# Making the rests of w1 and w2 with TensorE and ScalarE, and their signs with GpSimd, in a kernel of top-32 attention and a gated product

## The chip, the core and the metric

The kernel runs on one core of a Trainium2 chip. The metric is the time of one execution in microseconds (us) on the device. The engines are called PE (TensorE; PEld is its loading of weights), DVE (VectorE), ACT (ScalarE), POOL (GpSimd) and SP (SyncE, which issues the transfers here).

## The reference

```python
# q, k, v: (8, 8, 576, 64); x: (4608, 512); w1, w2: (512, 1024); w3: (1024, 1024); w_out: (1024, 512)
scores = q @ k^T / sqrt(64)
kth = np.partition(scores, -32, axis=-1)[..., -32:-31]
scores = np.where(scores >= kth, scores, -1e9)
attn = softmax(scores)                       # only the 32 largest of a row count
x = (attn @ v).transpose(0, 2, 1, 3).reshape(B * S, H * D)
out = ((x @ w1) * (x @ w2) @ w3) @ w_out
```

All inputs are random. The matrices w1, w2, w3 and w_out are handed to the device as 64-bit numbers, and the kernel turns them into 32-bit ones itself.

## The kernel before

**Slots.** The attention is cut into 144 slots, 18 for each of the 8 batches; a slot holds 128 rows of queries of two heads. The main loop takes slots through a software pipeline: in one turn of the loop PE makes the scores `st` of slot p+1, DVE finds the 32 largest of each row of slot p (`top`, working copy `w`), POOL and ACT mask and exponentiate slot p-1 (`edge`, `pab`, `sums`), and PE turns (`tp`, `ro`) and multiplies with the values (`ro`) for slot p-2. Each engine works through its instructions in the order in which the program states them.

**The product.** When the last slot of a part of a batch is through, its columns `xf` go through the four matrices: `moe_steps` states matmuls `ab` (x by w1 and w2) and `eo` (by the fold of w3 and w_out). Each matrix product is made of three: high part by high part, high by rest, rest by high. `fill(n)` states some 29 of these matmuls in a turn, at three places, and what is left over stands behind the last slot. `moe_steps` can't go on past `while done[f // 4] < NFC` before the weights of that half are there.

**Loading the weights.** Forty units of 128 x 512 numbers come in at the start: 8 of w_out, 16 of w3, 16 of w1 and w2. `startup` lists their order, and `warm` states one step of up to five units under way at up to four places of a turn, so the loading lies between the first slots. A unit's `decode` makes, from the upper words `high` of the 64-bit numbers, the shifted exponent and mantissa, and from the lower words `low` the last bits `r`. ACT does both conversions, DVE puts sign and shifted bits together in `y` (`scalar_tensor_tensor`), and POOL adds `r` (`y<-y,z`, or `wo<-y,z` for w_out). Where the flag `by_pool` is set, POOL made the signs into `y` first (`y<-z`); where it isn't, DVE did (`tensor_scalar`, `y<-t`). For w1 and w2 it isn't set. Behind that, `load_w12` has ACT copy `y` to the high part `wh`, and POOL subtracts for the rest `wl`. `load_w3` hands eight PE products (`pf`) to a list `heavy`, from which `weigh` states one or eight at two places of a turn.

**Memory.** The pool `ps_m` has three banks of PSUM; `ab`, `eo`, `pf` and the `t` of `decode` share them. `z` (the 64-bit numbers) has four buffers, and `y` and `xf` share nine. PE and ACT read PSUM's other banks for `st`, `tp` and `ro`.

All instructions go through a helper, so that nearly every row of the profile has line L52; the names tell them apart.

Of the kernel before, what the change touches and what calls it, by code (L numbers as in the profile page):

```python
# [9 lines left out]
F32 = mybir.dt.float32  # L10
F32R = mybir.dt.float32r
I32 = mybir.dt.int32
U16 = mybir.dt.uint16
AF = mybir.ActivationFunctionType
ALU = mybir.AluOpType
# [45 lines left out]
def attn_moe(ctx: ExitStack, tc: tile.TileContext, q, k, v, w1, w2, w3, w_out, out, flag, general):  # L61
# [11 lines left out]
    nc = tc.nc  # L73
    pe, act, dve, pool, sp = nc.tensor, nc.scalar, nc.vector, nc.gpsimd, nc.sync

    const = ctx.enter_context(tc.tile_pool(name="const", bufs=1))
# [9 lines left out]
    ps_m = ctx.enter_context(tc.tile_pool(name="ps_m", bufs=3, space=PSUM))  # L86

    ident = const.tile([128, 128], F32, name="ident")
    make_identity(nc, ident)
    coef = const.tile([128, 2, 2], F32, name="coef")  # L90
    pool.memset(coef[:, :, 0:1], -SCALE)
    pool.memset(coef[:, :, 1:2], STEEP)
# [11 lines left out]
    if not general:  # L104
        pe, act, dve, pool, sp = (InOrder(tc, e) for e in (pe, act, dve, pool, sp))
# [7 lines left out]
    def decode(z, by_pool, dst=None):  # L113

        y = x_p.tile([128, 2 * NA], F32, tag="x", name="y")[:, :512]
        high = z[:, 1:1024:2]  # L120
        low = z.bitcast(U16)[:, 1:2048:4]
        r, u = z[:, 0:1024:2].bitcast(I32), y.bitcast(I32)
        if by_pool:
            pool.tensor_scalar(y, high, 0.0, 1.0, op0=ALU.mult, op1=ALU.mult)
            yield
        t = ps_m.tile([128, 512], F32, tag="mm", name="t")
        act.activation(t, high, AF.Copy, scale=2.0**-112)
        act.activation(r, low, AF.Copy, scale=2.0**-13)
        yield
        ti = t.bitcast(I32)  # L130
        if not by_pool:
            dve.tensor_scalar(u, ti, -(2**31), None, op0=ALU.bitwise_and)
        dve.scalar_tensor_tensor(u, ti, 3, u, op0=ALU.logical_shift_left, op1=ALU.bitwise_or)
        yield
        dst = y if dst is None else dst
        pool.tensor_tensor(dst.bitcast(I32), u, r, op=ALU.add)
        yield
        return dst

    done = {"pf": 0, 0: 0, 1: 0}  # L140

    def load_w12(i, c, z):
        y = yield from decode(z, False)
        c, h = c // 2, c % 2
        if len(wl[i]) == h:
            while done["pf"] < NFC:
                yield
        if len(wl[i]) == h:
            wl[i].append(const.tile([128, half], F32R, tag="wl1", name="wl11"))
        y_hi, y_lo = wh[i][:, c * DF + h * 512 : c * DF + (h + 1) * 512], wl[i][h][:, c * 512 : (c + 1) * 512]  # L150
        act.copy(y_hi, y)
        yield
        pool.tensor_tensor(y_lo, y, y_hi.bitcast(F32), op=ALU.subtract)
        done[h] += 1

    def load_wout(c, z):
        yield from decode(z, c % 2, wo[:, c * 512 : (c + 1) * 512])

    fold, heavy = {}, []

    def weigh(n):
        while heavy and n:
            heavy.pop(0)()
            n -= 1

    def load_w3(c, z):
        f, i = c // 2, c % 2
        y = yield from decode(z, i)
        if i == 0:
            fold[f] = ps_m.tile([128, 512], F32, tag="mm", name=f"pf{f}")  # L170

        def product(j):
            pe.matmul(
                fold[f], y[:, (j % 4) * 128 : (j % 4 + 1) * 128], wo[:, j * DM : (j + 1) * DM],
                start=(j == 0), stop=(j == NFC - 1),
            )

        heavy.extend((lambda j=j: product(j)) for j in range(4 * i, 4 * i + 4))
        last = heavy[-1]
        if general:  # L180
            weigh(4)
        while last in heavy:
            yield
        if i == 1:
            cut = slice(f * DM, (f + 1) * DM)
            act.copy(wf[0][:, cut], fold[f])
            yield
            dve.tensor_tensor(wf[1][:, cut], fold[f], wf[0][:, cut].bitcast(F32), op=ALU.subtract)
            done["pf"] += 1
# [178 lines left out]
    def moe_steps(b, part, xs, after):  # L368
# [61 lines left out]
    thirds = [(w3[c], lambda z, c=c: load_w3(c, z)) for c in range(2 * NFC)]  # L430
    firsts = [
        (w[2 * c + h], lambda z, i=i, c=2 * c + h: load_w12(i, c, z))
        for h in range(2) for i, w in enumerate((w1, w2)) for c in range(NCC)
    ]
# [94 lines left out]
    for p in range(-1, n_slots + 3):  # L529
# [29 lines left out]
        if 0 <= j < n_slots:  # L559
            exps(edges[j], *pabs[j], 0)  # L560
            exps(edges[j], *pabs[j], 1)
        weigh(1)
        fill(SHARE[1])
        next(finder, None)
# [6 lines left out]
        if 0 <= m < n_slots:  # L571
            us, t = slots[m]
# [11 lines left out]
        if 0 <= j < n_slots:  # L584
            invert(pabs[j][1])
            normalise(*pabs[j])
        weigh(8)
        fill(SHARE[2])
        for _ in finder:
# [66 lines left out]
```

## Time and profile before

| | |
|---|---|
| time, median of 3 runs | 1272.27 us (1270.61 to 1272.45) |
| time of the profiled execution | 1272.79 us |
| its span, first to last instruction | 1270.8 us |
| mean granted TensorE clock, share of full | 0.988 |
| busy: PE / DVE / ACT / POOL | 1212.8 / 1135.0 / 942.9 / 870.2 us |

The time of an execution is 2.0 us longer than its span. A busy PE is not PE at its peak: matmuls are pipelined, and one that lasts 0.31 us may be followed by the next after half of that. So the text uses the distance from one start to the next where a price of PE is wanted.

### The profile page before, as it was taken

The page shows a single profiled execution, that of the slowest core. Times are in us where ns is not written, and L with a number is a line of the kernel's source. Part 1 is how long each engine was busy: PE and PEld are TensorE (multiplying, and loading weights), DVE is VectorE, ACT ScalarE, POOL GpSimd, SP SyncE. Part 2 cuts the span into 40 slices and gives each one's busy share as a digit, 9 for nine tenths or more (in the row PEclk, how much of TensorE's full clock was granted, in tenths as well). Part 3 has the DMA queues.
Part 4 walks back from the last instruction along what each step waited for, and adds up shares of the span by engine and source line. Part 5 has one row for each costly group of instructions (what it writes and reads, how often), then busy time and mean ns, then how long its engine had stood idle before and what let it go on. Part 6 is the DMA issues. An engine that isn't in the chain of part 4 may idle for free.

```text
span 1270.8 us, 29917 instructions
## 1 busy us (share of the span) xinstructions
PE 1212.8 (95%) x10513; PEld 1043.9 (82%) x10513; DVE 1135.0 (89%) x3968; ACT 942.9 (74%) x2025; POOL 870.2 (68%) x1213
## 2 busy tenths in 40 slices
PE   3788879999999999999999999999999999999998
PEld 1444468888888888888888888888888888888898
DVE  6898979999999999999999999999999999999910
ACT  6786767777777777777777777777777777777731
POOL 5887887676776667676676777676676767676731
PEclk9898989999999999999999999999999999999999
DMA  6444321212112021202112021202112111202000
GB/s 234 160 143 143 125 87 39 76 42 70 55 39 82 20 87 40 90 27 70 55 39 90 27 72 40 91 28 70 55 39 90 36 62 40 91 27 69 13 22 21
DMA packets 42803, 85.92 MB, mean 68 GB/s; under 512 B 4754, under 2 KB 21138, under 8 KB 42642
## 3 DMA queue, kind: packets, MB, share of 16 engines
q1 hardware_dynamic: 42642, 83.91, 20.3%
q8 instruction: 85, 1.39, 0.5%
q14 instruction: 76, 0.62, 0.2%
HBM read 74.45 MB, written 9.44 MB: 66 GB/s over the span
## 4 chain that ended last, share of the span: by engine, by line
PE 84%; POOL 8%; issue 2%; ACT 2%; DVE 2%; DMA 1%; SPq 0%; POOLq 0%; ACTq 0%; DVEq 0%
PE ab L52 31%; PE eo L52 16%; PE ro L52 14%; PE st L52 12%; PE tp L52 9%; POOL pab L52 4%; POOL y L52 2%; PE pf L52 2%; POOL wl L52 1%; DMA z<-in_wo 1%; ACT pab L52 1%; DVE w L52 1%; DVE top L52 1%; POOL g L52 0%; DVE y L52 0%
## 5 line engine op out<-in xcount | busy, mean ns | idle before, releaser
L52 POOL TENSOR_TENSOR pab<-s,pab 128x576 f32<-128x576 f32 x288 | 404.6, 1426 | 124.3 <-ACT pab L52 124.3
L52 DVE MAX8 top<-w 128x8 f32<-128x192 f32 (+1 forms) x1152 | 478.5, 448 | 0.0
L52 PE MATMUL ab<-xf,wh 128*128 128x256 f32 (+1 forms) x2048 | 438.9, 302 | 9.5 <-ACT asb L52 4.6
L52 PEld LDWEIGHTS ab<-xf,wh 128*128 128x128 f32 x2048 | 333.3, 189 | 21.0 <-issue 8.9
L52 ACT ACTIVATE pab<-s,edge 128x576 f32<-128x576 f32 x288 | 207.9, 770 | 174.9 <-POOL edge L52 174.9
L52 PE MATMUL ab<-xf,wl 128*128 128x256 f32 (+1 forms) x1024 | 307.6, 300 | 0.0
L52 DVE MATCH_REPLACE8 w<-top,w 128x192 f32<-128x192 f32 x864 | 289.7, 343 | 0.0
L52 POOL TENSOR_SCALAR pab<-pab,sums 128x576 f32<-128x576 f32 x288 | 211.7, 748 | 80.3 <-DVE sums L52 80.3
L52 ACT ACTIVATE pab<-pab,edge 128x576 f32<-128x576 f32 x288 | 223.2, 780 | 14.0 <-POOL pab L52 11.2
L52 PE MATMUL eo<-g,wf 128*128 128x256 f32 (+1 forms) x1536 | 231.6, 301 | 0.0
L52 PEld LDWEIGHTS eo<-g,wf 128*128 128x128 f32 x1536 | 208.5, 188 | 8.1 <-issue 7.5
L52 PEld LDWEIGHTS ab<-xf,wl 128*128 128x128 f32 x1024 | 193.5, 189 | 4.1 <-issue 4.1
L52 PE MATMUL st<-kt,qt 64*128 64x192 f32 (+3 forms) x1280 | 184.0, 436 | 11.4 <-DVE w L52 4.5
L52 ACT COPY pts<-tp 128x1024 f32<-128x1024 f32 x144 | 145.5, 1010 | 46.9 <-PE tp L52 44.5
L52 ACT COPY s<-st 128x768 f32<-128x768 f32 (+1 forms) x288 | 169.7, 645 | 0.0
L52 PEld LDWEIGHTS st<-kt,qt 64*128 64x128 f32 (+1 forms) x1280 | 98.2, 179 | 86.4 <-issue 18.7
L52 PE MATMUL tp<-ident,pab 128*128 128x128 f32 x1152 | 153.2, 277 | 15.5 <-POOL y L52 5.2
L52 DVE TENSOR_TENSOR w<-w,st 128x384 f32<-128x384 f32 x288 | 158.2, 549 | 4.9
L52 PE MATMUL ro<-pts,vt 128*64 128x128 f32 (+1 forms) x2560 | 161.6, 270 | 1.0 <-ACT pr L52 1.0
L52 DVE TENSOR_TENSOR w<-s,st 128x384 f32<-128x384 f32 x288 | 146.7, 551 | 14.0
L52 POOL TENSOR_TENSOR g<-whole,g 128x256 fp32r<-128x256 f32 (+1 forms) x128 | 103.0, 805 | 78.7 <-ACT g L52 78.7
L52 PEld LDWEIGHTS ro<-pts,vt 128*64 128x64 f32 x2560 | 127.9, 138 | 34.6 <-issue 24.0
(47 smaller groups left out, 1127.3 us busy)
## 6 DMA issues: line engine op xcount, KB each, us to landing
vt<-in_v SPq DMA_DIRECT2D x64, 352.0 KB, 3.1
kt<-in_k SPq DMA_DIRECT2D x64, 320.0 KB, 3.8
z<-in_w SPq DMA_DIRECT2D x32, 512.0 KB, 3.7
qt<-in_q SPq DMA_DIRECT2D x32, 160.0 KB, 3.1
out_t<-osb SPq DMA_DIRECT2D x32, 160.0 KB, 1.8
z<-in_wo SPq DMA_DIRECT2D x8, 512.0 KB, 5.8
qt<-in_q SPq DMA_DIRECT2D x32, 128.0 KB, 3.1
out_t<-osb SPq DMA_DIRECT2D x32, 128.0 KB, 1.7
```

What stands on the lines that cost most here:

```text
L52: ins = fn(*args, **kw)
```

## The change

The rest of a unit of w1 or w2 is no longer subtracted by POOL. A bank `rest` of `ps_m` receives two matmuls, the identity by `y` and a negated identity (`minus`, made once by ACT) by `wh`, and ACT copies `rest` to `wl`. The two matmuls go through `heavy`, like those of w3. The signs of w1 and w2 are made by POOL instead of DVE. And for all forty units ACT writes the converted upper words over themselves in `z` instead of into a bank `t`, so that `t` is gone and DVE reads `z`.

```diff
+    minus = const.tile([128, 128], F32R, name="minus")
+    nc.scalar.activation(minus, ident, AF.Copy, scale=-1.0)
...
-        t = ps_m.tile([128, 512], F32, tag="mm", name="t")
-        act.activation(t, high, AF.Copy, scale=2.0**-112)
+        act.activation(high, high, AF.Copy, scale=2.0**-112)
         act.activation(r, low, AF.Copy, scale=2.0**-13)
         yield
-        ti = t.bitcast(I32)
+        ti = high.bitcast(I32)
         if not by_pool:
             dve.tensor_scalar(u, ti, -(2**31), None, op0=ALU.bitwise_and)
         dve.scalar_tensor_tensor(u, ti, 3, u, op0=ALU.logical_shift_left, op1=ALU.bitwise_or)
...
     def load_w12(i, c, z):
-        y = yield from decode(z, False)
+        y = yield from decode(z, True)
...
         act.copy(y_hi, y)
         yield
-        pool.tensor_tensor(y_lo, y, y_hi.bitcast(F32), op=ALU.subtract)
+        rest = ps_m.tile([128, 512], F32, tag="mm", name="rest")
+
+        def subtract():
+            pe.matmul(rest, ident, y, start=True, stop=False)
+            pe.matmul(rest, minus, y_hi, start=False, stop=True)
+
+        heavy.append(subtract)
...
+        while subtract in heavy:
+            yield
+        act.copy(y_lo, rest)
         done[h] += 1
```

On POOL, this is the twelfth of the slots, between the `edge` of one slot and that of the next, before the change:

```order
L52 TENSOR_TENSOR edge<-top_100,coef 128x4
L52 TENSOR_TENSOR pab<-s,pab 128x576 x2
L52 TENSOR_TENSOR over<-top_100 128x2
L52 TENSOR_TENSOR wl_107<-y,wh_101 128x512
L52 TENSOR_TENSOR y<-y,z 128x512
L52 TENSOR_SCALAR sums<-sums 128x2
L52 TENSOR_TENSOR wl_107<-y,wh_101 128x512
L52 TENSOR_TENSOR y<-y,z 128x512
L52 TENSOR_SCALAR pab<-pab,sums 128x576 x2
```

and with the change:

```order
L52 TENSOR_TENSOR edge<-top_102,coef 128x4
L52 TENSOR_TENSOR y<-y,z 128x512
L52 TENSOR_TENSOR pab<-s,pab 128x576 x2
L52 TENSOR_TENSOR over<-top_102 128x2
L52 TENSOR_SCALAR y<-z 128x512
L52 TENSOR_TENSOR y<-y,z 128x512
L52 TENSOR_SCALAR sums<-sums 128x2
L52 TENSOR_SCALAR y<-z 128x512
L52 TENSOR_SCALAR pab<-pab,sums 128x576 x2
L52 TENSOR_TENSOR y<-y,z 128x512
```

Two subtractions are gone, two signs have come, and one sum of `y` more falls into this slot.

On PE, this is the eleventh slot's transposes and what follows them, where the matmuls `ab` have just begun, before the change:

```order
L52 MATMUL tp<-ident,pab 128x128 x8
L52 MATMUL ro<-ident,pab 128x128
L52 MATMUL ab<-xf,wh_101 128x320
L52 MATMUL ab<-xf,wl_106 128x320
L52 MATMUL ab<-xf,wh_102 128x320 x2
L52 MATMUL ab<-xf,wl_108 128x320
```

and with the change:

```order
L52 MATMUL tp<-ident,pab 128x128 x8
L52 MATMUL ro<-ident,pab 128x128
L52 MATMUL rest<-y,ident 128x512
L52 MATMUL rest<-wh_103,minus 128x512
L52 MATMUL ab<-xf,wh_103 128x320
L52 MATMUL ab<-xf,wl_108 128x320
L52 MATMUL ab<-xf,wh_104 128x320 x2
L52 MATMUL ab<-xf,wl_110 128x320
```

The two matmuls of a rest stand ahead of `ab`. Over the whole program the first `ab` stands in the same slot as before; eight rests stand ahead of it and eight among the `ab` of the four slots behind it. In the fourteenth slot of the change `moe_steps` comes to its second half before the weights are there: 20 matmuls `ab` are stated there and not 29. At the end 181 `eo` are left behind the last transposes, and 170 before.

## Rows read from the trace of the kernel before

**Rows 1.** The page's head: span, busy time by engine, chain by engine.

```profile
span 1270.8 us, 29917 instructions
PE 1212.8 (95%) x10513; PEld 1043.9 (82%) x10513; DVE 1135.0 (89%) x3968; ACT 942.9 (74%) x2025; POOL 870.2 (68%) x1213
PE 84%; POOL 8%; issue 2%; ACT 2%; DVE 2%; DMA 1%; SPq 0%; POOLq 0%; ACTq 0%; DVEq 0%
```

**Rows 2.** Busy time in five stretches, then clock, DMA share, GB/s.

```profile
0.00:33.80 33.80, 11.12 (x41) 4.80 (x41) 23.76 (x66) 19.31 (x33) 19.17 (x31) 0.97 0.69 235
33.80:150.00 116.20, 100.94 (x548) 54.81 (x548) 102.58 (x311) 90.94 (x179) 93.52 (x111) 0.92 0.44 147
150.00:200.00 50.00, 37.31 (x268) 30.89 (x269) 39.49 (x123) 34.75 (x71) 41.04 (x48) 0.93 0.25 79
200.00:1217.00 1017.00, 1015.03 (x9266) 905.59 (x9265) 964.58 (x3458) 787.15 (x1716) 709.84 (x1018) 1.00 0.17 55
1217.00:1271.00 54.00, 48.42 (x396) 47.80 (x394) 4.63 (x13) 10.77 (x27) 6.64 (x9) 0.97 0.08 25
```

**Rows 3.** PE in order of time, transposes of the first and the fifteenth slot: start, us, what.

```profile
33.78 1.94 PE L52 MATMUL tp<-ident,pab 128*128 128x128 f32 x8 [5.25 <-POOL y L52]
...
199.72 1.06 PE L52 MATMUL tp<-ident,pab 128*128 128x128 f32 x8 [0.72 <-DVE w L52]
```

**Rows 4.** The chain that ended last, by line, in 33.8:150 and in 150:200.

```profile
by line: PE pf L52 21.3%; POOL pab L52 20.3%; issue 16.7%; POOL y L52 14.6%; PE st L52 4.5%; PE ro L52 3.4%; ACT pab L52 2.7%; POOL wl L52 2.4%; ACT z L52 1.9%; ACT t L52 1.8%; PE tp L52 1.7%; ACT s L52 1.5%; DVE w L52 1.3%; POOL wo L52 1.1
...
by line: POOL pab L52 24.9%; POOL wl L52 20.0%; POOL y L52 17.6%; issue 11.5%; POOL g L52 6.8%; ACT pab L52 4.9%; ACT wh L52 2.9%; DVE y L52 2.8%; DVE top L52 2.7%; DVE w L52 2.1%; POOL over L52 0.9%; POOL sums L52 0.9%; POOL edge L52 0.8%;
```

**Rows 5.** Groups of the loading in the whole trace: busy, mean ns of one, idle before.

```profile
L52 POOL TENSOR_TENSOR wl<-y,wh 128x512 fp32r<-128x512 f32 x16 | 20.5, 1279 | 6.5 <-ACT wh L52 6.5
L52 POOL TENSOR_SCALAR y<-z 128x512 f32<-128x512 f32 x12 | 7.9, 656 | 11.0 <-DMA z<-in_wo 11.0
L52 DVE SCALAR_TENSOR_TENSOR y<-t,y 128x512 int32<-128x512 int32 x40 | 27.6, 689 | 6.5 <-POOL y L52 3.1 <-ACT xf L52 2.5
L52 DVE TENSOR_SCALAR y<-t 128x512 int32<-128x512 int32 x28 | 19.1, 683 | 17.8 <-ACT t L52 15.0 <-POOL y L52 2.8
L52 ACT ACTIVATE z<-z 128x512 int32<-128x512 uint16 x40 | 26.9, 673 | 0.0
L52 ACT ACTIVATE t<-z 128x512 f32<-128x512 f32 x40 | 25.8, 645 | 15.5 <-DMA z<-in_wo 9.7 <-DVE y L52 4.9 <-DMA z<-in_w 0.8
L52 ACT CAST wf<-pf 128x512 fp32r<-128x512 f32 x8 | 4.7, 587 | 9.8 <-PE pf L52 9.8
```

**Rows 6.** The chain in order of time, three pieces of PE: start, us, what.

```profile
95.81 6.22 PE pf L52 x14
...
311.74 1.48 PE ab L52 x10
...
315.62 3.13 PE ab L52 x20
```

**Rows 7.** POOL and DVE in order of time: two pairs that overlap.

```profile
16.05 0.68 DVE L52 SCALAR_TENSOR_TENSOR y<-t,y 128x512 int32<-128x512 int32 x1
14.54 2.53 POOL L52 TENSOR_TENSOR wo<-y,z 128x512 int32<-128x512 int32 x2
...
179.34 0.69 DVE L52 SCALAR_TENSOR_TENSOR y<-t,y 128x512 int32<-128x512 int32 x1
178.87 1.28 POOL L52 TENSOR_TENSOR y<-y,z 128x512 int32<-128x512 int32 x1
```

**Rows 8.** Who waited for whom up to 205: us in total, times, longest.

```profile
PE ab L52 <- DVE y L52: 3.2, 3, 1.6
```

**Rows 9.** PE in order of time, where it waits longest among the first `ab`.

```profile
157.49 0.31 PE L52 MATMUL ab<-xf,wl 128*128 128x320 f32 x1
162.43 0.90 PE L52 MATMUL ab<-xf,wh 128*128 128x320 f32 x2 [4.63 <-ACT asb L52]
163.13 0.47 PE L52 MATMUL ab<-xf,wl 128*128 128x320 f32 x1
```

More of the change, by code (lines that the diff above doesn't have):

```diff
@@ L140, in attn_moe, with weigh @@
     done = {"pf": 0, 0: 0, 1: 0}
+    fold, heavy = {}, []
+    def weigh(n):
+        while heavy and n:
+            heavy.pop(0)()
+            n -= 1
     def load_w12(i, c, z):
-        y = yield from decode(z, False)
+        y = yield from decode(z, True)
         c, h = c // 2, c % 2
@@ L152, in load_w12 @@
         yield
-        pool.tensor_tensor(y_lo, y, y_hi.bitcast(F32), op=ALU.subtract)
+        rest = ps_m.tile([128, 512], F32, tag="mm", name="rest")
[3 more added lines that the diff above has]
+        heavy.append(subtract)
+        if general:
+            weigh(1)
+        while subtract in heavy:
+            yield
+        act.copy(y_lo, rest)
         done[h] += 1
@@ L157, in load_wout @@
         yield from decode(z, c % 2, wo[:, c * 512 : (c + 1) * 512])
[L159 to L164, printed above, removed]
     def load_w3(c, z):
```

## The prediction

> **What bounds the kernel now.** The head of the page comes first: PE is busy 95% of the span and makes up 84% of the chain that ended last [rows 1]. That is an average, so the next view is the busy time by stretch [rows 2]. From 200 to 1217 us PE is busy 1015 of 1017 us at full clock; nothing on another engine can shorten that stretch. Before 200 us it is different: there the units of weights are loaded between the first slots, and no engine is full. The transposes of the first slot begin at 33.8 us and those of the fifteenth at 199.7 [rows 3], so a slot takes 11.9 us there; behind 200 us 129 slots take 1017 us, 7.9 us each. The change touches the loading alone. So its worth is what it does to the time at which PE becomes full, plus what PE work it pushes behind the last slot.
>
> In the first ten slots (33.8 to 150) DVE is the busiest with 102.6 of 116.2 us, PE follows with 100.9, POOL with 93.5, ACT with 90.9. In the next four (150 to 200) POOL is the busiest with 41.0 of 50.0 [rows 2]. The chain of these stretches says whose work is on the path [rows 4]. In the first, POOL has 20.3 + 14.6 + 2.4 + 1.1 = 38%, PE 21.3 + 4.5 + 3.4 + 1.7 = 31%, ACT 2.7 + 1.9 + 1.8 + 1.5 = 8%, DVE 1%. In the second POOL has 72%, a fifth of it the subtractions `wl`, ACT 8%, DVE 8%, and PE doesn't appear. I use these shares as weights: work added to or taken from an engine counts by the share that the engine has of the path there.
>
> **The change part by part.** *POOL.* Sixteen subtractions of 1.28 us go, sixteen signs of 0.66 us come [rows 5]. By the order seven subtractions and eight signs fall into the first ten slots, nine and eight into the next four. First: -7 x 1.28 + 8 x 0.66 = -3.7 us, weighted by 0.38 -1.4. Next: -9 x 1.28 + 8 x 0.66 = -6.2, by 0.72 -4.5.
>
> *PE.* A rest is two matmuls of 512 columns. For the identity by `y`, both in full 32 bits, the nearest row is `pf`: the trace has 128 instructions for 64 stated, so two each, and 14 take 6.22 us on the chain [rows 6], 0.44 each, 0.89 for the pair. For the negated one the nearest is `ab`, 20 of 320 columns in 3.13 us [rows 6]; scaled to 512 columns that is 0.25. Together 1.14 us, 18 us for sixteen. Eight stand in the first ten slots: 9.1 x 0.31 = +2.8. Eight stand among the first `ab`: PE idles 12.7 of the 50 us there [rows 2], enough for 9.1, so 0. With that cover gone it would be the 9.1.
>
> *ACT.* It copies a rest out of PSUM; the row is `wf<-pf`, the same size from the same pool, 0.59 us [rows 5]. Seven copies in the first ten slots are 4.1 x 0.08 = +0.3. In the next four come eight copies, and one more unit's two conversions (1.3 us): 6.0 x 0.08 = +0.5. Writing over `z` in place of PSUM is bounded by the two rows that differ in that, 0.67 against 0.65 [rows 5]: 40 x 0.03 = 1.1, 0.1 by weight, left out. The one negated identity is made before the first `z` is there, for which ACT waits (9.7 us in all for those of w_out [rows 5]), at nothing.
>
> *DVE.* Sixteen signs of 0.68 us go [rows 5], ten in the first ten slots and six in the next four, where one combination (0.69) more falls: -6.8 x 0.01 and -3.4 x 0.08, together -0.4. By busy time DVE is the fullest engine of the first ten slots; what follows if that decides is a rival below.
>
> *The end.* The half of the weights that comes last is ready about a slot later in the order, and eleven more matmuls are left behind the last transposes. Ten `ab` take 1.48 us [rows 6]: +1.6. Before 200 us they were no gain, since PE doesn't bound there.
>
> *Transfers.* All forty `z` are still loaded, three ahead. DMA engines are busy 44% and 25% in the two stretches [rows 2]; I count nothing.
>
> So far -1.4 - 4.5 + 2.8 + 0.3 + 0.5 - 0.4 + 1.6 = -1.1 us.
>
> *The combination reads two tiles of SBUF.* Before, `y<-t,y` took one operand from PSUM. So does every other two-operand instruction of DVE in the trace that works on scores or products. With the change all forty take `z` and `y`, both from the memory from which POOL works too. No row shows what this costs, so I bound it. Lower end: nothing, the 0.69 us stay. Upper end: an instruction of the one engine keeps the other out until it ends. Of the forty, 25 start in the middle of a POOL instruction; the first at 16.05 us inside `wo`, the last at 179.34 inside `y` [rows 7]. What was then left of POOL's instruction sums to 16.5 us. The other way round, in 21 cases POOL starts an instruction inside the combination, with 9.1 us left of it. If all of that came to the path, it would be 25.6 us. I weight it like the rest: of POOL's 9.1, 6.0 lie in the first ten slots (x 0.38 = 2.3) and 1.0 in the next four (x 0.72 = 0.7); DVE's 16.5 get 0.3, and the first 33.8 us, where transfers lead, 0.5. That is +3.8. I take it and not zero, because these overlaps are all that the rows say of the matter, and POOL was in the middle of an instruction at most of the forty starts.
>
> A rule on this is in the Trainium skill's "SBUF — State Buffer", section "Who interferes with whom": a DVE instruction with two SBUF inputs contends with a GpSimd instruction that reads SBUF, and whichever issues second is blocked until the first has finished. By that rule the sum ends at +2.7, without it at -1.1; no run so far shows the one or the other.
>
> -1.1 + 3.8 = +2.7 on the profiled execution's 1272.8, which is 0.5 above the median of the runs: 1275.5, less 0.5, **1275 us**.
>
> **The rivals.** *Exclusion isn't there, or is small, and the fullest engine decides (faster).* Then DVE's relief counts in the first ten slots (6.8 us) and POOL's in the next four (6.2), not by shares but as the bound. With the 1.6 of the end that is -11.4 at most; as the other engines are at 78 to 87% there, two thirds are likely: -7, **1265 us**. For it: the busy times [rows 2], and a fifth of the path of the four slots in subtractions alone [rows 4]. Also the banks: three waits of `ab` for the `t` of `decode`, 3.2 us [rows 8], disappear. Against: the chain gives DVE 1% of the first stretch. It decides if a combination stays at 0.69 us beside a busy POOL.
>
> *The rest's way is the new wait (slower).* Before, POOL made the rest as soon as `wh` stood. Now it goes through `heavy`, PE's queue, a bank of three and ACT's queue. Among the first `ab` there are eight rests, and a rest keeps its bank until ACT comes to the copy, behind masks and exponentials of the slot. Two tiles of `ab` later PE stands. That such waits are dear is seen at 157.8 to 162.4 us: PE waits 4.63 us for a copy of `asb`, and behind it three `ab` take 0.8 us, not 0.44, so the granted clock is at its lower level of 1.2 GHz for a while [rows 9]. If each of the eight costs what a `t` did, 3.2 / 3 = 1.07, and one more stall of 4.6 comes, it is 13 us, less the 3.2 of `t`: +10 on 1275, **1285 us**. It decides where ACT's copy comes later than two tiles of `ab` (24 x 0.15 = 3.6 us) after the rest. Against: PE idles a quarter of that stretch, and ACT is busy 35 of 50 us.
>
> *Neither exclusion nor relief*: the sum without its last term, -1.1, **1271 us**, no change that can be told.
>
> **How the numbers follow.** Forecast 0.45, of which its own range is 1270 to 1281; fullest engine 0.30 (1261 to 1270); the rest's way 0.15 (1280 to 1291); neither 0.10. A measurement of this kernel tells some 0.2% from no change, 2.5 us: below 1269.7 is faster, above 1274.8 slower. Faster: 0.45 x 0.05 + 0.30 x 0.9 + 0.10 x 0.1 = 0.30. Slower: 0.45 x 0.7 + 0.15 + 0.10 x 0.1 = 0.47. The rest, 0.23, is within. The range leaves out the outer half of the two outer rivals: **1263 to 1286**.
>
> **What would show it.** In the profile after: a combination `y<-z,y` whose mean is well above 0.69 us, or POOL instructions above 1.28 and 0.66 us at the same moments, say that exclusion is there; unchanged means refute it. PE's sixteen rests should add 18 us of busy time before 205 us, and ACT's copies some 9. Behind that time PE must be full again and a slot take 7.9 us. The start of the fifteenth slot's transposes, 199.7 us before, should come at 200 to 203 us, and the stretch behind the last transposes should be 1.6 us longer. The prediction is wrong if that start moves by more than 6 us either way: earlier with unchanged means is the first rival, later with waits of `ab` for ACT's copies the second.

## The result, and the profile after

The kernel of the change takes 1279.85 us in the median (five runs, 1277.07 to 1282.3) beside 1272.45 of the kernel before (1270.61 to 1274.53): ratio 1.0054, 95% interval 1.0036 to 1.0072. It is slower, and inside the forecast's range, but by 7.4 us where 2.7 were forecast. Its profiled execution took 1277.07 us, the fastest of the five.

The head of the page of the kernel after, then the chain that ended last by engine; they answer to [rows 1]:

```profile
span 1275.3 us, 30054 instructions
PE 1224.4 (96%) x10561; PEld 1047.0 (82%) x10561; DVE 1136.9 (89%) x3952; ACT 953.0 (75%) x2042; POOL 876.4 (69%) x1213
...
PE 63%; DVE 14%; POOL 10%; ACT 8%; issue 4%; DMA 0%; SPq 0%; DVEq 0%; ACTq 0%; POOLq 0%
```

PE is on 63% of the chain, 84% before; DVE went from 2% to 14%. A chain that leaves PE also behind the loading is the first sign that the slots themselves changed. Busy time by stretches, after, to be held against [rows 2] (the last stretch is longer):

```profile
0.00:33.80 33.80, 11.67 (x40) 5.09 (x40) 24.46 (x65) 18.55 (x32) 20.08 (x29) 0.96 0.66 231
33.80:150.00 116.20, 103.43 (x581) 56.24 (x582) 107.97 (x304) 95.95 (x189) 101.81 (x117) 0.98 0.43 148
150.00:200.00 50.00, 43.74 (x299) 34.05 (x297) 38.56 (x129) 41.67 (x85) 38.90 (x47) 0.97 0.24 83
200.00:1217.00 1017.00, 1012.97 (x9229) 900.12 (x9226) 960.50 (x3441) 784.69 (x1708) 706.34 (x1011) 1.00 0.17 54
1217.00:1275.30 58.30, 52.63 (x421) 51.51 (x420) 5.38 (x16) 12.18 (x32) 9.27 (x13) 0.98 0.07 23
```

In the first ten slots DVE is busy 108.0 us (102.6 before) although it lost ten signs, and POOL 101.8 (93.5) although subtractions left it: the first ten slots end 1.0 us earlier and six more POOL instructions fall into the stretch, and others got longer. From 200 to 1217 PE idles 4.0 us, 2.0 before, and runs 9229 instructions where it ran 9266.

Four marks cut the span into accounts: the transposes of the first, the fifteenth, the 32nd and the 144th slot. PE in order of time, after:

```profile
34.27 1.94 PE L52 MATMUL tp<-ident,pab 128*128 128x128 f32 x8 [7.24 <-DVE w L52]
...
196.47 1.04 PE L52 MATMUL tp<-ident,pab 128*128 128x128 f32 x8
...
331.18 1.03 PE L52 MATMUL tp<-ident,pab 128*128 128x128 f32 x8
...
1219.70 1.38 PE L52 MATMUL tp<-ident,pab 128*128 128x128 f32 x8
```

and the last two of the kernel before, whose first two stand in [rows 3]:

```profile
334.32 1.03 PE L52 MATMUL tp<-ident,pab 128*128 128x128 f32 x8
...
1217.31 1.03 PE L52 MATMUL tp<-ident,pab 128*128 128x128 f32 x8
```

| us | before | after | difference |
|---|---|---|---|
| start of the fifteenth slot | 199.7 | 196.5 | -3.2 |
| 15th to 32nd slot | 134.6 | 134.7 | +0.1 |
| 32nd to 144th slot | 883.0 | 888.5 | +5.5 |
| behind the last transposes | 53.5 | 55.6 | +2.1 |
| span | 1270.8 | 1275.3 | +4.5 |

The loading ended earlier and the kernel is slower all the same: 5.5 us came in 112 slots in which no weight is loaded and which the prediction left at 7.9 us each. That was not foreseen. A second profile of the same kernel (below) has 200.2, 134.7, 888.6 and 55.5: the loading differs from one execution to the next, the steady part doesn't.

The groups of the loading, after, for [rows 5]:

```profile
L52 DVE SCALAR_TENSOR_TENSOR y<-z,y 128x512 int32<-128x512 int32 x40 | 40.1, 1002 | 10.4 <-ACT z L52 9.8
L52 POOL TENSOR_TENSOR over<-top 128x2 f32<-128x2 f32 x144 | 32.0, 222 | 0.0
L52 ACT ACTIVATE z<-z 128x512 f32<-128x512 f32 x40 | 27.6, 690 | 18.8 <-POOL y L52 13.2 <-DMA z<-in_wo 5.4
L52 PE MATMUL rest<-y,ident 128*128 128x512 f32 x32 | 16.6, 602 | 0.8 <-ACT wl L52 0.8
L52 PE MATMUL rest<-wh,minus 128*128 128x512 f32 x16 | 12.7, 796 | 0.0
L52 ACT CAST wl<-rest 128x512 fp32r<-128x512 f32 x16 | 9.5, 591 | 0.3
```

The combination, 689 ns before, has a mean of 1002. How that comes about is seen in DVE's order of time at 57 us, after:

```profile
57.39 1.58 DVE L52 TENSOR_SCALAR y<-z 128x512 int32<-128x512 int32 x1
59.00 1.79 DVE L52 SCALAR_TENSOR_TENSOR y<-z,y 128x512 int32<-128x512 int32 x1
```

and POOL's at the same moment:

```profile
57.27 2.97 POOL L52 TENSOR_TENSOR pab<-s,pab 128x576 f32<-128x576 f32 x2
60.20 0.64 POOL L52 TENSOR_TENSOR over<-top 128x2 f32<-128x2 f32 x1
```

The two `pab` of 1.4 and 1.6 us end at 58.68 and 60.24. DVE's sign, begun inside the first, ends some 0.3 us behind it; the combination, begun inside the second, ends at 60.79, 0.55 behind it; and `over`, 0.2 us as a rule, is held to 60.84, when the combination is through. Each waits until the other's instruction has ended. That is the rule that the prediction took from the Trainium skill, "SBUF — State Buffer", section "Who interferes with whom": the trace agrees, in both directions, and the same section names `tensor_scalar`, under conditions on its operands, among the operations that can be caught so, which the sign shows and the prediction had not counted.

One slot of the steady part shows where most of its 5.5 us come from. PE at the turn to the 35th slot, after:

```profile
354.81 0.31 PE L52 MATMUL ab<-xf,wl 128*128 128x320 f32 x1
355.47 0.96 PE L52 MATMUL tp<-ident,pab 128*128 128x128 f32 x7 [0.36 <-DVE w L52]
```

and DVE just before it:

```profile
353.38 0.17 DVE L52 RECIPROCAL sums<-sums 128x2 f32<-128x2 f32 x1 [0.78 <-POOL sums L52]
353.46 0.74 DVE L52 MAX8 top<-w 128x8 f32<-128x576 f32 x1
354.31 1.02 DVE L52 TENSOR_TENSOR w<-s,st 128x384 f32<-128x384 f32 x2
```

DVE, which reads `st` out of PSUM for its `w` (in this kernel PE writes those banks, and ACT and DVE read them), stood 0.78 us for POOL's sum, so its `w` ends at 355.33, and PE's transposes wait for it. This slot (347.10 to 355.47) takes 8.37 us and not 7.86, and in each of the six whole batches of the stretch the same one of the 18 slots does; the next takes 8.12. Over a batch that is 142.86 us against 142.14, +0.72. The 112 slots hold six whole batches, 4.3 us, and four slots behind them, which take 1.2 us more than before; together that is the 5.5.

### The profile page after: what moved, and what is told of

Same layout as the page of the kernel before. It is cut to its first block, busy times and chain, and to the rows that moved or that the text cites. A ratio compares the mean times of both kernels' runs of the same rounds, so it can differ in the third digit from the quotient of the medians.

```text
span 1275.3 us, 30054 instructions
## 1 busy us (share of the span) xinstructions
PE 1224.4 (96%) x10561; PEld 1047.0 (82%) x10561; DVE 1136.9 (89%) x3952; ACT 953.0 (75%) x2042; POOL 876.4 (69%) x1213
## 4 chain that ended last, share of the span: by engine, by line
PE 63%; DVE 14%; POOL 10%; ACT 8%; issue 4%; DMA 0%; SPq 0%; DVEq 0%; ACTq 0%; POOLq 0%
PE ab L52 19%; PE eo L52 17%; PE ro L52 10%; PE st L52 9%; PE tp L52 7%; POOL pab L52 7%; DVE w L52 6%; DVE top L52 4%; ACT pab L52 3%; DVE y L52 2%; POOL g L52 2%; ACT z L52 1%; ACT s L52 1%; POOL y L52 1%; ACT pts L52 1%
## 5 line engine op out<-in xcount | busy, mean ns | idle before, releaser
L52 PE MATMUL ab<-xf,wh 128*128 128x256 f32 (+1 forms) x2048 | 434.1, 301 | 5.7 <-ACT asb L52 5.7
L52 POOL TENSOR_SCALAR pab<-pab,sums 128x576 f32<-128x576 f32 x288 | 215.1, 760 | 74.5 <-DVE sums L52 74.5
L52 PEld LDWEIGHTS tp<-ident,pab 128*128 128x128 f32 x1152 | 130.0, 141 | 32.4 <-POOL edge L52 17.2
```

Source lines behind the costliest of these rows:

```text
L52: ins = fn(*args, **kw)
```

## The experiments

Differences are of medians to the kernel before beside it. The table is in the order of the argument; start means that of the fifteenth slot's transposes in the profile. A start belongs to one execution, whose time lies up to 3.8 us from the median of its row (signs on POOL 1263.72 us, the bank 1272.76, all forty signs 1274.58, early signs 1267.6), so starts of two rows tell less than their medians.

| kernel | time, us | ratio (95%) | diff. | start | 32nd to 144th | behind |
|---|---|---|---|---|---|---|
| before | 1272.0 to 1272.5 | | | 199.7 | 883.0 | 53.5 |
| the change | 1279.85 | 1.0054 (1.0036 to 1.0072) | +7.4 | 196.5 | 888.5 | 55.6 |
| the change again | 1280.66 | 1.0058 (1.0045 to 1.0072) | +8.7 | 200.2 | 888.6 | 55.5 |
| before, eleven matmuls later | 1276.94 | 1.0030 (1.0018 to 1.0042) | +4.6 | 200.6 | 885.7 | 55.4 |
| change, caught up in turns | 1277.9 | 1.0045 (1.0031 to 1.0058) | +5.6 | 196.5 | 883.3 | 53.8 |
| before, converted in place | 1287.85 | 1.0118 (1.0103 to 1.0134) | +15.6 | 215.7 | 883.1 | 53.5 |
| change with the bank `t` | 1274.86 | 1.0016 (1.0007 to 1.0026) | +2.6 | 192.1 | 888.5 | 55.4 |
| that, caught up at once | 1270.22 | 0.9982 (0.9973 to 0.9991) | -1.8 | 193.4 | 883.3 | 53.5 |
| that, caught up in later turns | 1267.59 | 0.9966 (0.9955 to 0.9978) | -4.5 | 192.1 | 883.0 | 53.6 |
| before, rests alone | 1275.27 | 1.0031 (1.0018 to 1.0043) | +3.2 | 201.9 | 883.4 | 53.6 |
| before, signs on POOL alone | 1265.93 | 0.9952 (0.9938 to 0.9966) | -6.1 | 190.2 | 883.4 | 53.7 |
| before, signs early on DVE | 1263.81 | 0.9929 (0.9915 to 0.9942) | -8.1 | 194.5 | 883.0 | 53.5 |
| before, a step more | 1265.11 | 0.9933 (0.9918 to 0.9948) | -6.8 | 192.3 | 882.9 | 53.7 |
| before, all forty signs on POOL | 1272.51 | 0.9999 (0.9989 to 1.0009) | +0.6 | 201.4 | 883.0 | 53.6 |

**The eleven matmuls alone.** The kernel before, but in one turn eleven matmuls are not stated, so that from there on the product stands as far back as in the change.

```diff
-        fill(SHARE[1])
+        fill(SHARE[1] - (11 * 352 if p == 15 else 0))
```

> The kernel before with nothing but eleven matmuls of the product stated later: in the fourteenth slot 18 are stated and not 29, as with the change. Theory A (the lag of eleven matmuls costs in every batch): from the fifteenth slot's transposes to the last slot's 1023 us as with the change, not 1017.6; 2 us more behind the last transposes, at most 1.6 us won in the fourteenth slot: 1277 to 1279 us. Rival B (the price of the change lies in the loading, by the combination or by the rests' waits): that stretch stays at 1017.6, and the time rises by at most 1.6: 1272 to 1274 us.

It lost 4.6 us by the medians. In the profiles 2.7 are in the steady part, 1.9 behind it, and 0.9 at the start, which is no more than two executions of one kernel differ by (below). So a lag alone costs in every batch. It gives half of the 5.5: the slot that takes 8.37 us with the change takes 8.10 here. The order differs from the change's by one matmul in some turns; that this is the reason isn't shown.

**The change, caught up.** One matmul more in each of eleven turns.

```diff
-        fill(SHARE[1])
+        fill(SHARE[1] + (352 if 17 <= p < 28 else 0))
```

> The changed kernel, but eleven turns of the main loop behind the loading state one matmul of the product more, so that from there on the order is that of the kernel before. Theory A: the stretch from the 36th slot on is again as before, the end 2 us shorter, 1.6 us given in the eleven turns: some 6 us under the changed kernel, 1271 to 1274 us. Rival B: no more than 1 us is won: 1277 to 1280 us.

The steady part is back at 883.3 us, as expected; the time is not, because the eighteenth slot now takes 11.71 us. PE there:

```profile
221.73 1.72 PE L52 MATMUL eo<-g,wf 128*128 128x320 f32 x10
225.33 0.57 PE L52 MATMUL eo<-g,wf 128*128 128x320 f32 x1 [1.87 <-POOL g L52]
225.82 2.20 PE L52 MATMUL st<-kt,qt 64*64 64x384 f32 x16
```

It met the passage from `ab` to `eo`, where the last rest of `g` wasn't ready, 1.87 us, and behind that wait `st` was slower (granted clock 0.52 from 225.33 to 228 us, the lower level for nearly all of it), which cost some 2 us more.

**In place alone.** The kernel before with the conversions in place, nothing else.

```diff
-        t = ps_m.tile([128, 512], F32, tag="mm", name="t")
-        act.activation(t, high, AF.Copy, scale=2.0**-112)
+        act.activation(high, high, AF.Copy, scale=2.0**-112)
...
-        ti = t.bitcast(I32)
+        ti = high.bitcast(I32)
```

> The kernel before with the conversion in place alone; the order is the same. If DVE and POOL keep each other out (theory P): the combination's mean is about 1.0 us as with the change, not 0.69, DVE has 12 us more in the loading, the fifteenth slot's transposes begin 3 to 8 us later than at 199.7, and everything behind it is as before: 1275 to 1280 us. Rival Q (the longer combination of the changed kernel comes from somewhere else, such as the rests): 0.69 us and 1272 us. In both cases the stretch behind the fifteenth slot stays at 1017.6.

Its groups:

```profile
L52 DVE SCALAR_TENSOR_TENSOR y<-z,y 128x512 int32<-128x512 int32 x40 | 43.4, 1084 | 9.6 <-ACT z L52 8.7
...
L52 ACT ACTIVATE z<-z 128x512 f32<-128x512 f32 x40 | 27.2, 680 | 26.6 <-POOL y L52 20.6 <-DMA z<-in_wo 5.9
```

The combination is longer by 0.40 us, forty times; and the conversion, which now writes `z`, waits 20.6 us for POOL to have read it, a wait that stands nowhere in [rows 5]. The start moves by 16.0 us, twice what was expected at most. What of it is the combination, what the new wait and what the signs that DVE now reads from `z`, these runs don't separate.

**The change with the bank.** The change, with `t` in PSUM as before.

```diff
-        act.activation(high, high, AF.Copy, scale=2.0**-112)
+        t = ps_m.tile([128, 512], F32, tag="mm", name="t")
+        act.activation(t, high, AF.Copy, scale=2.0**-112)
...
-        ti = high.bitcast(I32)
+        ti = t.bitcast(I32)
```

> The changed kernel with the converted upper words in a bank of PSUM again, as before the change; the order is that of the change. Theory P: the combination is back at 0.69 us, POOL's small instructions are back at 0.2 us, and the fifteenth slot's transposes begin 3 to 8 us earlier than with the change. Theory A at the same time: the stretch behind them stays at 1023 us, so 1271 to 1276 us in all. Rival Q, and a rival R (with the rests in the three banks, the conversions must wait for them): the start is no earlier or later, 1277 to 1284 us.

```profile
L52 DVE SCALAR_TENSOR_TENSOR y<-t,y 128x512 int32<-128x512 int32 x40 | 27.5, 687 | 12.0 <-ACT t L52 11.6
...
L52 ACT ACTIVATE t<-z 128x512 f32<-128x512 f32 x40 | 26.0, 649 | 9.9 <-DMA z<-in_wo 7.6 <-DVE w L52 1.4 <-DVE wf L52 0.7
```

In these groups the combination is back at 687 ns and the wait for POOL is gone. The start comes at 192.1, 4.4 us (8.1 in the second profile of the change) earlier, and the steady part keeps its 888.5; by the medians the bank is worth 4.8 to 6.1 us. So in place and lag are two separate losses.

**That, caught up in two ways.** At once, six and five matmuls in two turns:

```diff
-        fill(SHARE[1])
+        fill(SHARE[1] + {19: 6 * 352, 20: 5 * 352}.get(p, 0))
```

> The kernel with the rests on TensorE and the signs on GpSimd, the converted words in a PSUM bank; two turns in which only eo is stated (the fillings of slots 18 and 19) state six and five matmuls more, so that from there on the order of the product is that of the kernel before. Theory A (a lag of eleven matmuls costs in every batch): from the 32nd to the 144th slot 883 us and not 888.5, behind the last transposes 53.4 and not 55.4; start of the fifteenth slot 192.1 as without the edit; the eleven matmuls cost 1.6 us once. Sum 192.1 + 134.7 + 1.6 + 883.1 + 53.4 = 1265, so a time of 1266 to 1269 us, ratio 0.995 to 0.998. Rival B (the steady loss belongs to the rests themselves, as by other places in memory): 888 there, 1275 us. A new wait at the place of catching up, as in the run that caught up in turns from slot 17 on (3.9 us), would give 1270 to 1272.

or one in each of eleven turns, later than in the run above:

```diff
-        fill(SHARE[1])
+        fill(SHARE[1] + (352 if 20 <= p < 31 else 0))
```

> As the kernel that catches up at once, but with one matmul more in each of eleven turns, from the twentieth on, behind the first eo. Theory A: the same 883 us from about the 32nd slot on, 1266 to 1269 us. Rival B: 888 and 1275 us. If catching up in small steps meets a wait of eo for g again, 3 to 4 us more between the fifteenth and the 32nd slot: 1270 to 1272 us.

PE in order of time, the bank kept and caught up in turns; the first row is the fifteenth slot, then the 32nd and the 144th:

```profile
192.13 1.04 PE L52 MATMUL tp<-ident,pab 128*128 128x128 f32 x8
...
328.86 1.03 PE L52 MATMUL tp<-ident,pab 128*128 128x128 f32 x8
...
1211.88 1.03 PE L52 MATMUL tp<-ident,pab 128*128 128x128 f32 x8
```

883.0 us between the last two, as before the change: the lag was the cause of the steady loss, and the rests and their places in memory were not. Without it the time falls by 7.0 us (+2.6 to -4.5; 5.3 between the two profiles, in which the catching up takes 2.0 us back) and is below that of the kernel before. Caught up at once it meets a wait of `eo` for `g` again (1.61 us) and gains less.

**The rests alone.** The kernel of the bank with the signs on DVE again, `decode(z, False)`. A rest brings its unit a step more too, in `while subtract in heavy: yield`.

> The rests alone: on TensorE and ScalarE as in the change, signs on VectorE as before, converted words in a bank as before. The order of the product is then that of the kernel before from the 14th slot on: no lag. Theory A: 883 us from the 32nd to the 144th slot. By the weights of the prediction the start of the fifteenth slot moves by -7 x 1.28 x 0.38 - 9 x 1.28 x 0.72 + 2.8 + 0.8 = -8 us to 191.6, time 1264 to 1267 us. By the fullest engine (DVE in the first ten slots keeps its signs) only the four slots behind them gain: start at 194 to 198, time 1267 to 1271 us. If the steady loss belongs to the rests and not to the lag: 888 us, and 5 us more.

The fifteenth slot here:

```profile
201.94 1.03 PE L52 MATMUL tp<-ident,pab 128*128 128x128 f32 x8
```

Start at 201.9, not at 191.6: the weights of the prediction say 8 us earlier, the chip 2.2 later. In the last four slots before it, where the subtractions were weighted at 8.3 us, the time went from 49.6 to 51.4 us. The chain by line from 33.8 to 150 us:

```profile
by line: PE pf L52 36.9%; PE ro L52 8.7%; PE st L52 7.9%; ACT pab L52 6.7%; issue 5.6%; DVE y L52 4.1%; PE tp L52 3.9%; ACT pts L52 3.9%; ACT t L52 3.8%; ACT z L52 3.2%; PE rest L52 2.8%; DVE w L52 2.3%; DVE top L52 2.3%; POOL y L52 2.2%; A
```

POOL, 38% of the path in [rows 4], has nearly left it, and the lines of PE shown make up 60%. That PE's coming up is what took the gain away is argued, not shown. POOL also waits 23.5 us for ACT's `pab` before 205 us here, 10.5 in the kernel before, and the step more in each unit was not tried apart from the rest.

**The signs alone, in three forms.** On POOL (`decode(z, True)` in `load_w12`, nothing else), which gives each unit one step more, since POOL's sign has a `yield` of its own behind it:

> The signs alone: on GpSimd, with the rests subtracted by GpSimd as before, converted words in a bank as before; order of the product as before. By the weights of the prediction GpSimd's 8 x 0.66 x 0.38 + 8 x 0.66 x 0.72 less VectorE's 0.4 make the fifteenth slot start 5.4 us later, at 205: 1277 to 1279 us. By the fullest engine VectorE's 6.8 us count in the first ten slots and GpSimd's 5.3 in the next four, so the start moves by -2 to +1 us: 1270 to 1274 us. Both: 883 us from the 32nd to the 144th slot.

Then the sign at that place but on DVE, `(dve if by_pool == 2 else pool).tensor_scalar(...)`:

> The kernel before, with the signs of w1 and w2 made by VectorE still, but from z and one step earlier, in the place where GpSimd makes them in the run of the signs alone. Each is some 0.68 us of VectorE as before, but none waits for ScalarE's conversion. Theory V (the signs alone gained 9.5 us at the start of the fifteenth slot because 16 x 0.68 us of VectorE's work left): start at 198 to 201 us, 1271 to 1274 us. Rival W (they gained because VectorE no longer stood at a sign until ScalarE's conversion was there): start at 190 to 193, 1264 to 1267 us. Rival X (one step more to a unit spreads the loading better): the same 190 to 193, told from W by the run with the step alone.

And the step with nothing in it, all signs where they were:

```diff
-        if by_pool:
+        if by_pool == 1:
             pool.tensor_scalar(y, high, 0.0, 1.0, op0=ALU.mult, op1=ALU.mult)
+        if by_pool:
             yield
...
-        if not by_pool:
+        if by_pool != 1:
...
-        y = yield from decode(z, False)
+        y = yield from decode(z, 2)
```

> The kernel before with one empty step more in each unit of w1 and w2, where GpSimd's sign stands in the run of the signs alone; the signs stay on VectorE behind the conversions. Rival X (the step does it): start of the fifteenth slot at 190 to 193 us, 1264 to 1267 us. Theory V and rival W: 198 to 202, 1271 to 1276 us. Order of the product as before, so 883 us from the 32nd to the 144th slot.

The fifteenth slot with the signs on POOL, then with the step alone:

```profile
190.19 1.06 PE L52 MATMUL tp<-ident,pab 128*128 128x128 f32 x8 [0.71 <-DVE w L52]
...
192.27 1.07 PE L52 MATMUL tp<-ident,pab 128*128 128x128 f32 x8 [0.71 <-DVE w L52]
```

All three are faster than before by 6 to 8 us, and their intervals overlap. The empty step is enough for it: rival X, without the work taken off DVE and without the wait taken off it. The early sign on DVE even became dearer in the mean, with its operands in SBUF (0.68 us each before); the sixteen take from 0.41 to 1.68 us:

```profile
L52 DVE TENSOR_SCALAR y<-z 128x512 f32<-128x512 f32 x16 | 13.7, 859 | 0.0
```

With the step, the same instructions stand on the same engines, in another order: a unit's conversion, combination, sum, copy and subtraction come later in the turns. Two groups of the kernel with the step show one thing that became better:

```profile
L52 POOL TENSOR_TENSOR wl<-y,wh 128x512 fp32r<-128x512 f32 x16 | 20.5, 1280 | 1.5 <-ACT wh L52 1.4
...
L52 ACT CAST wh<-y 128x512 fp32r<-128x512 f32 x16 | 10.0, 627 | 5.2 <-POOL y L52 5.2
```

POOL waited 6.5 us at `wl` for ACT's `wh` before [rows 5], and ACT, in the kernel before:

```profile
L52 ACT CAST wh<-y 128x512 fp32r<-128x512 f32 x16 | 10.0, 624 | 12.6 <-POOL y L52 12.6
```

Fewer such waits back and forth go with the gain, but that they are the gain isn't shown: the rests alone take POOL's wait away too, leave 5.1 us of ACT's, and gain nothing. The chain from 33.8 to 150 us in the kernel with the step:

```profile
by line: PE pf L52 18.9%; issue 10.3%; POOL pab L52 8.2%; DVE w L52 7.7%; ACT pab L52 6.5%; PE tp L52 5.4%; DVE y L52 5.2%; PE ro L52 4.6%; ACT t L52 4.4%; POOL y L52 4.3%; DVE top L52 4.2%; ACT pts L52 3.3%; PE st L52 3.0%; ACT s L52 2.8%;
```

`pab` on POOL has fallen from 20.3 to 8.2% and `y` from 14.6 to 4.3, with not an instruction more or less. That this is the gain isn't shown either: with the signs on POOL, which gains as much, the same stretch has

```profile
by line: POOL pab L52 15.7%; POOL y L52 12.9%; issue 11.5%; PE pf L52 10.7%; ACT pab L52 7.8%; DVE w L52 5.0%; ACT pts L52 4.8%; POOL wl L52 4.4%; ACT s L52 3.7%; DVE top L52 3.5%; DVE y L52 3.5%; ACT z L52 3.3%; ACT t L52 2.7%; PE ro L52 2
```

and POOL still stands at 33%. PE's granted clock differs as well: from the first slot to the eleventh it is 0.92 before [rows 2], 0.94 with the step (33.88 to 146.13 us) and 0.98 with the signs on POOL (32.99 to 140.97), and the same instructions keep PE busy 100.9, 98.1 and 94.1 us. Whether the clock is part of the gain or follows from shorter waits stays open. That the step is worth 6.8 us is shown; which wait it shortens to that end isn't.

**All forty signs on POOL**, that is the same flag in `load_wout` and `load_w3` too:

> The signs of all forty units on GpSimd, nothing else changed. Twelve signs more leave VectorE, mostly before and in the first ten slots. If VectorE's relief goes on counting as it did for the sixteen (9.5 / 16 = 0.6 us each), the fifteenth slot starts up to 7 us earlier than with the sixteen alone: 183 to 187 us, 1258 to 1262 us. If GpSimd, busy for 108.6 of 117 us there with the sixteen, is now the fullest: 190 to 198 us, 1265 to 1272 us.

Start at 201.4, 11.2 us behind the kernel of sixteen, later than either account said; the medians are 6.6 us apart, and 1272.51 us lies half a us above the second account. Whether POOL's load or twelve more steps do it stays open.

**The change again:**

> The kernel of the change once more, since its profiled execution was the fastest of its five and its median 2.8 us above it. The time: 1277 to 1281 us. If the spread lies in the loading, a second profile has the start of the fifteenth slot elsewhere than at 196.5 us by about as much as its time differs; if in the steady part, its 888.5 us differ.

The steady part repeats to 0.1 us. The start is 3.7 us later, 0.4 before the first slot and 1.6 in each of two slots. PE at the first of them, in the profile above:

```profile
90.88 1.07 PE L52 MATMUL tp<-ident,pab 128*128 128x128 f32 x8 [3.11 <-DVE w L52]
...
91.89 1.02 PE L52 MATMUL rest<-y,ident 128*128 128x512 f32 x2
```

and in the second one:

```profile
91.35 1.57 PE L52 MATMUL tp<-ident,pab 128*128 128x128 f32 x8 [3.11 <-DVE w L52]
...
92.93 1.91 PE L52 MATMUL rest<-y,ident 128*128 128x512 f32 x2
```

The wait is the same 3.11 us; behind it one execution has the full clock of 2.4 GHz (granted 1.00 from 90.88 to 95 us) and the other falls to the lower one of 1.2 GHz (0.62 from 91.35 to 93 us, 0.50 from there to 95). The medians of the two series, 1279.85 and 1280.66 us, lie nearer the second (1280.83) than the first (1277.07).

## Why the prediction was right, and where it was so by chance

Range and direction held: 1279.85 us, 1280.66 in the second series, with 1275 forecast and the forecast's own range ending at 1281. The size didn't: +7.4 and +8.7 where +2.7 was forecast, and in the profiles 7.6 us of it lie in the steady part and behind the last transposes, where 1.6 was forecast. The account held in part. The chain of kernels before, a step more, signs on POOL, rests (caught up), lag, in place leads from the one kernel to the other; medians give -6.8, then +0.7, +1.7, +7.0 and +4.8 to +6.1. The second and third are within what the intervals leave open, and in another order the parts are worth other sums (the rests alone +3.2, in place alone +15.6). The lag belongs to no single part: with the rests alone and with the signs alone every slot has the matmuls of the product that it has before, and 170 `eo` are left at the end; only both together make the units late enough for eleven matmuls to fall behind.

- *Work weighted by shares of the chain* (in sum -2.7; DVE's -0.4 is -0.3 by its own products): this step failed. By it the rests alone are worth -8.1 and the signs alone +5.4 (the expectations of those runs work it out); the start moved by +2.2 and -9.5, the medians by +3.2 and -6.1. The two errors stood against each other in one sum, which is why the forecast of the start came near: that is luck. Both parts together, in the kernel of the bank, moved the start by -7.6. A share says who was on the path in this order; with the rests alone PE stood on it in POOL's place, and with the empty step POOL's share fell without any work moved.
- *A step of a unit counts nothing.* The prediction counted POOL's signs as 0.66 us each and not that each brings one `yield` more for its unit. Alone on the kernel before, an empty step in its place is worth 6.8 us, more than any other gain among the parts.
- *The prices of single instructions* held: a rest takes 1.18 us on PE (91.89 to 93.07 us, from its first matmul to the next `st`), forecast 1.14; ACT's copy 0.591, forecast 0.59. PE's busy time grew by 11.6 us over the span and not by the 18 named as a sign, while its granted clock from 33.8 to 150 us was 0.98 and not 0.92.
- *The combination reads two tiles of SBUF*: the mechanism is right. Mean 1002 ns, POOL's instructions longer at the same moments, both named as the signs to look for. Its size, +3.8, is not measured by itself: +4.8 to +6.1 in time is all of in place, and the same edit alone on the kernel before costs 15.6. Not foreseen were that the conversion in place waits for POOL's reading of `z` (13.2 us) and that DVE's signs are caught too.
- *The end*, eleven matmuls, +1.6: mis-sized by what it left out. Behind the last transposes 2.1 us were measured; but the lag that puts the matmuls there shifts the product against the slots in every batch, 5.5 us more. "Behind that time PE must be full again and a slot take 7.9 us" was wrong for two slots of a batch. That the lag is the cause is shown by catching up, which gives 883.0 us again.
- *Start of the fifteenth slot at 200 to 203*: 196.5 and 200.2 in two profiles, the second the more usual.
- *Rival "fullest engine"*: it hung on a combination of 0.69 us; that fell. With the empty step all signs stay on DVE, and that kernel is as fast as the one with the signs on POOL, so what came earlier there was not DVE's relief.
- *Rival "the rest's way"*: matmuls of a rest waited 0.8 us in all for ACT, and `ab` 5.4 us for `asb`, 4.6 before; it fell. *"Neither"* fell with the combination.

The best version tried keeps the kernel before and adds the empty step or the early sign on DVE: ratios 0.9933 and 0.9929. Neither was tried together with the rests on PE.

## What to carry to other kernels

A price weighted by an engine's share of the chain had the wrong sign for both parts that were run alone here; the path moves when work moves, so each part of such a change needs its own run. Where work is stated in turns by a budget, look at what a delay in one place does to the phase of everything behind it, and where a `yield` stands is an edit of its own. A tile moved from PSUM to SBUF can make two engines wait for each other though they work on different tiles at that moment, and writing it in place adds a wait for whoever still reads the source.

## What the runs showed of the hardware

- A DVE instruction with two operands in SBUF beside POOL's took up to 1.79 us in the rows above instead of 0.69, and POOL's `over`, 0.2 us, took 0.64 behind it. DVE's sign with its operands in SBUF took 1.58 us beside POOL's `pab`; the shortest of the twelve in the same trace took 0.41.
- After the same idle time of 3.11 us PE had the full clock in one execution and the lower level in another; with a second such place, behind a wait of 2.04 us for `asb` in both, that makes 3.2 of the 3.7 us by which the starts differ. The busy times of the stretch from 89 to 95 us in the first profile of the change, with the granted clock in the third column from the end:

```profile
89.00:95.00 6.00, 4.12 (x34) 2.88 (x36) 5.86 (x16) 5.50 (x10) 5.73 (x9) 1.00 0.55 184
```

and in the second:

```profile
89.00:95.00 6.00, 3.65 (x12) 2.29 (x12) 5.86 (x16) 4.68 (x8) 5.75 (x7) 0.73 0.65 214
```
